# A two-headed sequence kernel: the shift weights' cast and the small diagonals moved from GpSimd to VectorE, with a new order of all steps

## The chip, the cores and the metric

The kernel runs on one core of a Trainium2 chip. The core has five engines that run side by side: TensorE (matmuls), VectorE, ScalarE, GpSimd and SyncE, which here only starts transfers. The metric is the device time of one execution in microseconds (us); smaller is better. The profiled span of an execution is about 1.8 us shorter than its timed value (259.0 against 260.8 us before). Runs are called fast or slow by their time and by the clock that was granted to TensorE, and only fast runs are compared.

## The reference

The output is the concatenation of two independent layers, each over 2048 time steps and 640 channels in bf16.

```python
# Part A: diagonal state space model (complex, 640 states)
Lam_bar = exp(dt * (Lambda_re + 1j * Lambda_im))
B_bar   = ((Lam_bar - 1) / Lam)[:, None] * (B_re + 1j * B_im)
h[t]    = Lam_bar * h[t-1] + B_bar @ x[t]            # t = 0 .. 2047
y[t]    = 2 * real(C @ h[t]) + Dskip * x[t]
# Part B: a short convolution, a gate, a long convolution, a gate
k_shift = sum over j in 0..3 of shift_k[:, j] * k delayed by j
kv      = k_shift * v
y       = irfft(rfft(kv padded to 4096) * rfft(ssm_k padded))[:2048] + ssm_D * kv
out_b   = q * y
out     = concatenate([out_a, out_b], axis=-1)
```

## The kernel before

Both parts are cut into small steps, and one long string, `ORDER`, says in which sequence they are issued. Each name is a Python generator. Each time that the name occurs, the generator advances by one step, and the instructions that the step emits are chained in that order on their engine. An engine therefore runs its instructions strictly in the order of the string. An instruction that waits holds up everything behind it on the same engine.

```python
last, running, traced, at = {}, {}, nc.cur_bb.bb.instructions, 0
for name in ORDER.split():
    if name not in running:
        kind = name.rstrip("0123456789")
        running[name] = makers[kind](*(int(d) for d in name[len(kind):])) or iter(())
    next(running[name], None)
    for ins in traced[at:]:
        if last.get(ins.engine, ins) is not ins:
            tc.add_manual_dep(ins, last[ins.engine].name, ...)      # cut
        last[ins.engine] = ins
    at = len(traced)
```

The step names that matter below are these.

- Part A: `xt` turns x, `dg` makes small diagonal matrices, and `bt` and `lb` turn rows of B plainly and through those diagonals. `m(c,j)` is a block: 20 matmuls of 128x512 and a scan on VectorE, for time half c and state group j. `c` scales C, and `k` makes the constant matrix K0. `p(c,i,e)` is an output product: about 30 matmuls, one evacuation of PSUM on ScalarE and one store. It needs nothing more from VectorE.
- Part B, for each of five channel groups G: `v` convolves on VectorE, `sh` and `sk` are the first transform stage, `h` and `f` the spectra (with the products on VectorE), `z` goes back, `zt` or `zp` turns, `y` finishes and multiplies by q, and `st` stores. `R`, `g` and `Mq` build the transform constants, and `tb` builds tables.

The four places that the change touches:

```python
def start(self):                                   # Part B, first thing on GpSimd
    g = self.nc.gpsimd
    g.memset(self.dtap[:], 0.0)
    ...                                            # cut: one small load
    sk_b = self.small.tile([128, 5, 4], bf16, name="sk_b")
    g.dma_start(out=sk_b[:], in_=self.B_shift_k.rearrange("(g c) j -> c g j", c=128))
    g.tensor_copy(out=self.sk[:], in_=sk_b[:])     # waits here for the load above

def make_dg(self, j):                              # three 128x128 diagonals of row j
    eng = self.nc.vector if j == 0 else self.nc.gpsimd
    for i, v in enumerate((self.ndim, self.dre, self.dim)):
        eng.tensor_scalar_mul(out=self.dg[:, j, i, :], in0=self.ident[:], scalar1=v[:, j:j + 1])

def turn_lb(self, j):                              # uses them on TensorE
    ...
            nc.tensor.matmul(pl[:, k - k0, :], lhsT=bre[:, ks], rhs=dg[:, 1:3, :], start=True, stop=False)
            nc.tensor.matmul(pl[:, k - k0, :], lhsT=bim[:, ks], rhs=dg[:, 0:2, :], start=False, stop=True)
    ...

# ORDER: first line ... last two lines (553 steps in all)
# xl0 bl3 xl1 g0 bl2 bl4 R kl0 rot g0 dg0 dg2 bt3 cl Mq dg1 R rot tb2 bt3 Mq dg3 tb2 Mq xt3 bl0 xt2 gs xt3 ...
# p101 f44 z42 p101 z41 z43 z42 ql4 p110 z43 zp40 p110 zp41 zp40 zp42 p110 zp41 zp43 zp42 p111 zp43 y41 p111 y40 y41 p130 p111 y40 st4 p131
# p130 p130 p120 p131 p131 p121 p120 p120 p121 p121
```

The last two lines show that before ends with eleven steps of output products alone (behind `st4`).

## Time and profile before

Four runs of before gave 260.18, 260.52, 261.64 and 782.32 us; the last one is counted as slow.

| stretch of the profiled run, us | length | TensorE busy | VectorE busy | what sets the pace |
|---|---|---|---|---|
| 0 to 30.4 | 30.4 | 9.6 | 9.7 | waits for constants and diagonals |
| 30.4 to 64.9 | 34.6 | 25.0 | 28.6 | blocks, one late row of B |
| 64.9 to 95.5 | 30.6 | 28.1 | 30.0 | VectorE |
| 95.5 to 240 | 144.5 | 135.3 | 118.1 | mostly TensorE |
| 240 to 259 | 19.0 | 15.4 | 2.4 | TensorE alone |

These are the first lines of the profile page of before: busy time of each engine, then the busy tenths of 40 equal slices of the span, then each engine's share of the chain of waits that ended last (in before this chain could be followed back only to 95.5 us, so its shares add up to 62% of the span). PE is TensorE, PEld its weight loads, DVE VectorE, ACT ScalarE, POOL GpSimd.

```profile
PE 213.4 (82%) x2207; PEld 160.0 (62%) x2207; DVE 188.7 (73%) x355; ACT 168.9 (65%) x232; POOL 40.9 (16%) x89
...
PE   0223949668999787999999999999997899799994
...
POOL 4099994332021000000000000000000000000000
...
PE 31%; DVE 23%; ACT 5%; issue 3%; DVEq 0%; ACTq 0%
```

TensorE starts late (twos in the first slices, where GpSimd is at 9) and is full at the end. The windows of before, from which the table is taken, give the stretch in this form: length, then busy time of PE, PEld, DVE, ACT and POOL with instruction counts, then granted clock, DMA share and GB/s.

```profile
95.50:240.00 144.50, 135.29 (x1591) 107.61 (x1591) 118.08 (x212) 99.96 (x117) 0.22 (x2) 1.00 0.67 141
```

The start is explained by GpSimd's timeline in before (start, duration, engine, line, operation, result and sources; in brackets the idle time before it and what ended it).

```profile
2.98 0.91 POOL L575 DMA_DIRECT2D sk_b<-in_B_shift_k_dram  x1
12.67 0.20 POOL L576 CAST sk<-sk_b 128x20 f32<-128x20 bf16 x1 [8.78 <-DMA sk_b<-in_B_shift_k_dram]
...
16.47 0.61 POOL L334 TENSOR_SCALAR dg<-ident,ndim 128x128 bf16<-128x128 bf16 x1
...
32.60 2.02 POOL L334 TENSOR_SCALAR dg<-ident,ndim 128x128 bf16<-128x128 bf16 x1
34.60 2.05 POOL L334 TENSOR_SCALAR dg<-ident,dre 128x128 bf16<-128x128 bf16 x1
36.64 1.60 POOL L334 TENSOR_SCALAR dg<-ident,dim 128x128 bf16<-128x128 bf16 x1
```

GpSimd stands still for 8.78 us before a cast of 0.20 us, because it waits for a load that it started itself. A diagonal takes 0.6 us there, and the last three (row 4) take 1.6 to 2.05 us. The timeline of TensorE in before shows who pays for this.

```profile
23.77 0.37 PE L356 MATMUL pl<-dg,nat_re 128*128 128x256 bf16 x1 [9.37 <-POOL dg L334]
...
30.37 1.25 PE L468 MATMUL ps<-xe_110,BT 128*128 128x512 bf16 x5 [0.52 <-DVE xe_110 L316]
...
38.30 0.27 PE L356 MATMUL pl<-dg,nat_re 128*128 128x256 bf16 x1 [3.42 <-POOL dg L334]
```

TensorE waits 9.37 and 3.42 us for diagonals, and the first matmul of a block starts at 30.37 us. The end of before, in the timeline of ScalarE, is the evacuation of the last output product; its store follows, and the span ends at 259.0.

```profile
255.51 0.69 ACT L541 CAST yo<-ps 128x640 bf16<-128x640 f32 x1 [3.38 <-PE ps L537]
```

Three marks are used: the start of the first 128x512 block matmul (30.4 us in before), of the first K0 product on TensorE (69.3) and of the first spectrum product on VectorE (95.5). What is left from the third mark to the end is called *the rest*; in before it is 259.0 - 95.5 = 163.5 us.

### The profile page before, as it was taken

What the parts mean: (1) busy time and instruction counts of PE and PEld (TensorE: products, weight loads), DVE (VectorE), ACT (ScalarE), POOL (GpSimd) and SP (SyncE); (2) the same over time, 40 slices, a digit from 0 to 9 for tenths busy, and PEclk for the clock granted to TensorE, in tenths of its full rate; (3) what the DMA queues carried; (4) which work ended last, traced back from release to release, by engine and by line L of the source; (5) the groups of instructions that cost most, each with busy time, mean ns of one, the idle gap of its engine ahead of it and who ended that gap; (6) DMA issues with size and microseconds to landing.
All of it is one profiled execution on the core that took longest, in us unless ns stands there. A gap on an engine that the chain in (4) does not pass through costs nothing.

```text
span 259.0 us, 5361 instructions
## 1 busy us (share of the span) xinstructions
PE 213.4 (82%) x2207; PEld 160.0 (62%) x2207; DVE 188.7 (73%) x355; ACT 168.9 (65%) x232; POOL 40.9 (16%) x89
## 2 busy tenths in 40 slices
PE   0223949668999787999999999999997899799994
PEld 0212724334576576666778788876956788688772
DVE  3312793998999999999999459769899991942300
ACT  5045627998769888675546288767977998464221
POOL 4099994332021000000000000000000000000000
PEclk9999999968999999999999999999999999999999
DMA  5989908100007999691099450699579469171321
GB/s 155 213 176 242 244 8 209 34 1 3 0 0 103 194 205 220 143 210 35 25 262 192 113 132 3 196 180 219 112 153 230 109 132 188 41 172 37 89 71 51
DMA packets 101760, 33.03 MB, mean 127 GB/s; under 512 B 97256, under 2 KB 100584, under 8 KB 101736
## 3 DMA queue, kind: packets, MB, share of 16 engines
q1 hardware_dynamic: 101636, 32.68, 59.7%
q8 instruction: 17, 0.28, 0.5%
q0 software_dynamic: 80, 0.01, 0.2%
q14 instruction: 7, 0.06, 0.1%
q10 hardware_dynamic: 20, 0.00, 0.0%
HBM read 10.82 MB, written 7.86 MB: 72 GB/s over the span
## 4 chain that ended last, share of the span: by engine, by line
PE 31%; DVE 23%; ACT 5%; issue 3%; DVEq 0%; ACTq 0%
PE ps L524 15%; DVE pr L492 4%; PE ps L537 3%; DVE pw L683 3%; DVE pw L684 2%; DVE tap L640 2%; DVE tap L646 2%; DVE po L481 2%; DVE pr L481 2%; ACT Xs L679 2%; DVE Y L685 1%; ACT Hf L665 1%; DVE qin L744 1%; DVE Y L686 1%; PE ps L587 1%
## 5 line engine op out<-in xcount | busy, mean ns | idle before, releaser
L524 PE MATMUL ps<-C_183,h 128*128 128x320 bf16 x320 | 48.4, 299 | 1.3 <-DVE qin L744 0.7
L524 PEld LDWEIGHTS <-h 128*128 128x128 bf16 x320 | 30.4, 98 | 12.4 <-issue 1.8
L541 ACT CAST yo<-ps 128x640 bf16<-128x640 f32 x16 | 11.1, 694 | 33.5 <-PE ps L537 15.6
L679 ACT CAST Xs<-ps 128x1024 bf16<-128x1024 f32 (+1 forms) x25 | 21.8, 895 | 5.6 <-DVE pw L684 5.4
L589 ACT CAST As_h<-ps 128x1024 bf16<-128x1024 f32 x20 | 19.4, 1033 | 4.0 <-PE ps L587 4.0
L665 ACT CAST Hf<-ps 128x1024 bf16<-128x1024 f32 (+1 forms) x25 | 20.8, 910 | 1.2 <-PE ps L608 1.1
L716 ACT CAST Zs<-ps 128x1024 bf16<-128x1024 f32 x20 | 19.8, 1038 | 1.8 <-PE ps L714 1.8
L683 DVE TENSOR_TENSOR pw<-Xs,Hf 128x1024 bf16<-128x1024 bf16 (+1 forms) x25 | 15.2, 607 | 7.4 <-ACT Xs L679 7.4
L589 ACT CAST As_kv<-ps 128x1024 bf16<-128x1024 f32 x20 | 19.2, 1062 | 1.5 <-PE ps L587 1.5
L646 DVE TENSOR_TENSOR tap<-tap 128x2048 bf16<-128x2048 bf16 x15 | 19.1, 1273 | 0.5
L468 PEld LDWEIGHTS <-BT 128*128 128x128 bf16 x100 | 9.7, 100 | 14.7 <-issue 3.4
L470 PEld LDWEIGHTS <-BT 128*128 128x128 bf16 x100 | 10.0, 100 | 12.6 <-issue 1.4
L605 PE MATMUL ps<-As_h,Gre 128*128 128x128 bf16 x75 | 16.4, 219 | 1.7 <-ACT Hf L665 1.1
L474 ACT CAST z<-ps 128x1024 bf16<-128x1024 f32 x10 | 10.1, 1014 | 11.1 <-PE ps L470 11.1
L356 PE MATMUL pl<-dg,nat_re 128*128 128x256 bf16 x25 | 6.6, 300 | 12.8 <-POOL dg L334 12.8
L711 PE MATMUL ps<-Y,Hre 128*128 128x128 bf16 x75 | 16.4, 219 | 0.3 <-ACT As_kv L589 0.3
L608 PE MATMUL ps<-As_kv,Gre 128*128 128x128 bf16 x75 | 16.4, 219 | 0.0
L605 PE MATMUL ps<-As_kv,Gre 128*128 128x128 bf16 x75 | 16.4, 219 | 0.0
L607 PE MATMUL ps<-As_kv,Gim 128*128 128x128 bf16 x75 | 16.4, 219 | 0.0
L606 PE MATMUL ps<-As_kv,nGim 128*128 128x128 bf16 x75 | 16.4, 219 | 0.0
L714 PE MATMUL ps<-Y,Hre 128*128 128x128 bf16 x75 | 16.4, 219 | 0.0
L608 PE MATMUL ps<-As_h,Gre 128*128 128x128 bf16 x75 | 16.4, 219 | 0.0
(234 smaller groups left out, 652.3 us busy)
## 6 DMA issues: line engine op xcount, KB each, us to landing
h_st<-in_B_ssm_k_dram SPq DMA_DIRECT2D x5, 512.0 KB, 4.7
qin<-in_B_q_dram SPq DMA_DIRECT2D x5, 512.0 KB, 6.7
kv_d<-vT SPq DMA_DIRECT2D x5, 512.0 KB, 3.1
kv_st<-kv_d SPq DMA_DIRECT2D x5, 512.0 KB, 4.0
out_dram<-yo SPq DMA_DIRECT2D x16, 160.0 KB, 1.8
out_dram<-qin SPq DMA_DIRECT2D x5, 512.0 KB, 4.0
nat_re<-in_A_B_re_dram SPq DMA_DIRECT2D x5, 160.0 KB, 4.5
nat_im<-in_A_B_im_dram SPq DMA_DIRECT2D x5, 160.0 KB, 4.8
```

The source lines that it names most:

```text
L524: nc.tensor.matmul(py[:, b, 0:320], lhsT=h[:, s, hs], rhs=self.C4[:, 2 * e + s, j, c0:c0 + 320], start=(j == 0 and s == 0), stop=False)
L589: nc.scalar.copy(out=As[:, :, 32 * pr:32 * pr + 32], in_=pf.rearrange("p (c k) -> p k c", k=32))
L605: nc.tensor.matmul(pt[:, 0, cs], lhsT=C.Gre[:, k1, :], rhs=As[:, r, :], start=True, stop=False)
L606: nc.tensor.matmul(pt[:, 0, cs], lhsT=C.nGim[:, k1 - 1, :], rhs=As[:, im, :], start=False, stop=True)
L607: nc.tensor.matmul(pt[:, 1, cs], lhsT=C.Gim[:, k1, :], rhs=As[:, r, :], start=True, stop=False)
L608: nc.tensor.matmul(pt[:, 1, cs], lhsT=C.Gre[:, k1, :], rhs=As[:, im, :], start=False, stop=True)
L646: nc.vector.tensor_tensor(out=acc[:], in0=acc[:], in1=t[:], op=ALU.add)
L665: nc.scalar.copy(out=S["Hf"][:, :, pos * 128:(pos + n) * 128], in_=pt[:, :, 0:n * 128])
L679: nc.scalar.copy(out=Xs[:, :, 0:W], in_=pt[:, :, 0:W])
L683: nc.vector.tensor_tensor(out=pw[:, 0, :, 0:W], in0=Xs[:, :, 0:W], in1=Hf[:, :, hs], op=ALU.mult)
L711: nc.tensor.matmul(o_re, lhsT=C.Hre[:, k1, :], rhs=ypl(k1, 0), start=True, stop=False)
L716: nc.scalar.copy(out=Zs[:, :, 8 * qd:8 * qd + 8], in_=pzf.rearrange("p (k c) -> p c k", k=8))
```

## The change

Its intent is to get GpSimd's chain of waits off the start: the small loads are issued first, index rows (iotas) follow while they fly, the cast of the shift weights becomes a step `sc` of VectorE, and the 12 diagonals of rows 1 to 4 join those of row 0 on VectorE. Some of Part A's scalars come later, and the whole string of steps is new.

```diff
 ORDER = """
-xl0 bl3 xl1 g0 bl2 bl4 R kl0 rot g0 dg0 dg2 bt3 cl Mq dg1 R rot tb2 bt3 Mq dg3 tb2 Mq xt3 bl0 xt2 gs xt3 lb3 bl1 xt2 xt3 hl0 xt2 bt2 lb3 xt1
+xl0 bl0 xl1 bl4 kl0 g0 R Mq g0 bl1 rot dg0 Mq bl3 bt0 rot dg2 dg1 lb0 tb0 cl Mq bt0 R Mq gs tb0 lb0 xt3 xt1 sc xt3 xt3 xt4 dg3 bl2 xt0 xt1
 ...   (all 553 steps reordered to 556; cut)
-p101 f44 z42 p101 z41 z43 z42 ql4 p110 z43 zp40 p110 zp41 zp40 zp42 p110 zp41 zp43 zp42 p111 zp43 y41 p111 y40 y41 p130 p111 y40 st4 p131
-p130 p130 p120 p131 p131 p121 p120 p120 p121 p121
+f41 f40 y31 p111 f41 y30 f42 p111 y31 f43 p111 f42 f44 z40 st3 f43 f42 p110 z40 f44 f43 z41 p110 f44 z42 p110 z41 z43 ql4 z42 p130 z43 zp40
+p130 zp41 zp40 zp42 p130 zp41 zp43 zp42 zp43 y40 y40 y41 y41 st4
 """
@@ make_dg @@
-        eng = self.nc.vector if j == 0 else self.nc.gpsimd
         for i, v in enumerate((self.ndim, self.dre, self.dim)):
-            eng.tensor_scalar_mul(out=self.dg[:, j, i, :], in0=self.ident[:], scalar1=v[:, j:j + 1])
+            self.nc.vector.tensor_scalar_mul(out=self.dg[:, j, i, :], in0=self.ident[:], scalar1=v[:, j:j + 1])
@@ g_scalars @@
+        yield                                     # diagD later
         self.diagD = self.const.tile([128, NT, 128], bf16, name="diagD")
@@ PartB.start @@
-        g.tensor_copy(out=self.sk[:], in_=sk_b[:])
+    def cast_sk(self):                            # step "sc"
+        self.nc.vector.tensor_copy(out=self.sk[:], in_=self.sk_b[:])
@@ kernel body @@
     C.start()
+    pb.start()
     pa.preamble()
-    pb.start()
+    C.iotas()                                     # index rows gathered in one method
```

Cut: the moves of iotas into one method, one iota removed, and one more `yield` in `Mq`.

More of the change, by code (lines that the diff above doesn't have):

```diff
@@ L32 @@
 ORDER = """
-xl0 bl3 xl1 g0 bl2 bl4 R kl0 rot g0 dg0 dg2 bt3 cl Mq dg1 R rot tb2 bt3 Mq dg3 tb2 Mq xt3 bl0 xt2 gs xt3 lb3 bl1 xt2 xt3 hl0 xt2 bt2 lb3 xt1
-bt2 bt4 xt1 xt1 lb2 bt4 xt4 lb2 xt0 xt4 tb1 ql0 xt0 xt4 xt0 v0 dg4 tb1 m02 R tb3 v0 tb3 v0 lb4 g2 m02 m03 v0 lb4 m02 v0 g2 m02 m04 c40 tb0
-c00 c40 c20 c40 lb1 c00 c30 c00 c01 lb1 m02 bt1 c01 bt0 c20 bt1 tb0 kl1 c01 m01 c20 c10 g1 c30 c30 m03 c31 g1 bt0 lb0 c41 c21 g4 c31 lb0 m01
-c31 m00 c41 c10 c10 c21 c11 c41 c11 ht0 c21 k4 m01 g4 c11 k2 g3 k4 m01 m00 g3 k3 m01 g5 k2 sh00 k3 sh01 m00 sh02 sh00 sh03 sh02 v0 m00 k0 g5
@@ L37 @@
-tb4 sh03 H k1 sh01 m00 tb4 v1 sk00 k0 sk01 sk00 sk02 sk01 v1 late xb1 sk03 sk02 h00 sk03 v1 h01 h00 k1 f00 v1 hl1 h01 f01 m03 f00 v1 f02 f01
-f03 m04 f04 f00 h02 h02 f01 h03 f02 h04 f03 f02 z00 h03 h04 f03 f04 z01 z00 xb1 z01 m10 f04 m03 kl2 z02 m10 ht1 m03 sh10 z02 z03 sh11 sh10
-sh12 m10 sh13 z03 v1 m14 sh13 zt0 m10 sh11 sh12 m10 h10 m14 h11 m04 h10 h12 h11 h13 m04 h12 h14 m13 h13 h14 m04 sk10 m13 sk11 v2 p011 sk11
-sk10 v2 y01 p011 v2 y00 sk12 p011 sk13 sk12 hl2 y01 p001 sk13 y00 v2 st0 m14 v2 f10 p001 f11 f10 p001 ht2 m14 sh20 f11 f12 sh20 f13 f14 f10
@@ L41 @@
-ql1 p021 kl3 f12 f11 f13 f12 p020 p021 p021 f14 f13 p010 p020 p020 f14 sh21 sh22 sh21 sh23 v2 p000 sh23 sh22 p010 p010 h20 m14 p000 h21 h20
-p000 h22 h21 v3 h23 h22 h24 sk20 h23 sk21 sk22 h24 sk21 p030 v3 sk22 sk20 v3 z10 p030 z11 v3 p030 z10 z12 m13 z11 v3 z13 z12 sk23 p031 m13
-z13 hl3 sk23 zt1 m13 kl4 f20 p031 f21 f20 f22 ht3 f21 f20 f23 p031 f24 m11 f22 f21 f23 f22 sh30 f24 f23 sh31 m11 sh32 sh33 sh30 f24 v3 y11
-sh32 m11 z20 sh31 z21 sh33 y11 y10 z20 h30 y10 z21 h31 h30 m11 st1 h32 h31 h33 h32 h34 z22 m11 h33 sk30 h34 sk31 z22 sk32 v4 sk33 sk31 hl4
@@ L45 @@
-z23 sk32 ql2 m12 sk33 v4 sk30 z23 v4 zt2 f30 ht4 v4 m12 f31 f30 m12 f32 v4 f31 f33 f34 f30 sh40 sh40 sh41 f32 f31 sh42 sh41 sh43 sh42 f32
-y21 f33 v4 z30 sh43 f33 z31 f34 z30 y20 z31 f34 z32 y21 h40 z32 z33 y20 h40 h41 z33 m12 st2 h42 h41 zt3 h43 h42 h44 m12 h43 sk40 sk41 sk40
-sk42 sk43 sk41 ql3 p100 sk43 sk42 h44 f40 p100 f41 f40 p100 f42 f41 f40 y30 y31 f43 f42 f41 f44 y30 f43 z40 y31 p101 z40 f42 st3 f44 f43 z41
-p101 f44 z42 p101 z41 z43 z42 ql4 p110 z43 zp40 p110 zp41 zp40 zp42 p110 zp41 zp43 zp42 p111 zp43 y41 p111 y40 y41 p130 p111 y40 st4 p131
@@ L49 @@
-p130 p130 p120 p131 p131 p121 p120 p120 p121 p121
+xl0 bl0 xl1 bl4 kl0 g0 R Mq g0 bl1 rot dg0 Mq bl3 bt0 rot dg2 dg1 lb0 tb0 cl Mq bt0 R Mq gs tb0 lb0 xt3 xt1 sc xt3 xt3 xt4 dg3 bl2 xt0 xt1
+xt1 hl0 xt4 xt2 xt4 dg4 tb1 ql0 bt4 xt0 xt0 xt2 lb4 xt2 bt4 gs tb1 m00 lb4 v0 tb4 bt1 v0 m00 lb1 R tb4 m04 bt1 v0 tb2 lb1 tb2 v0 m00 lb3 v0
+tb3 m04 bt3 lb3 m01 m00 tb3 g2 c40 c40 bt3 bt2 c30 c40 lb2 bt2 c20 m03 c30 c30 c10 c20 c20 c00 c10 c10 c00 m03 kl1 c00 g2 ht0 k2 m00 g5 lb2
+m03 sh00 k2 sh01 sh00 k0 m03 sh01 g5 sh02 sh03 m03 v0 g1 k0 k4 sh02 sh03 m04 g1 k3 m04 g4 m01 k4 sk00 k3 sk01 m02 g4 m04 g3 sk01 m01 sk00 g3
@@ new lines @@
+sk02 m01 sk03 k1 hl1 sk03 H m02 h00 m01 sk02 h01 k1 h02 h00 m02 h03 h01 h04 f00 h02 ht1 late xb1 m02 f01 h03 h04 sh10 f00 f02 f01 f03 sh10
+m02 sh11 sh12 sh11 sh13 sh12 f00 p000 sh13 f02 f01 f04 p010 p000 c41 f03 p000 v1 c41 z00 p010 v1 p030 p010 z00 xb1 c41 c21 m11 p030 v1 c21
+p030 v1 c11 v1 c21 m10 c11 c01 f02 m11 c01 kl2 c11 z01 f04 f03 m10 m14 z01 f04 v1 c31 c01 c31 m10 z02 z03 z02 m10 h10 z03 h11 h10 zt0 h12
+m10 m14 h13 h11 h14 p020 h12 v2 h13 h14 v2 sk10 p020 sk11 sk12 sk10 p020 sk13 v2 m12 sk11 hl2 sk13 v2 sk12 m11 v2 y00 y01 m12 c31 f10 y00
@@ new lines @@
+f11 f10 kl3 f12 y01 f11 f13 ht2 f10 sh20 p031 sh20 f11 f12 st0 f13 f12 f14 sh21 p031 sh22 sh21 p031 sh23 f13 v2 p021 sh23 sh22 m11 f14 f14
+z10 p021 m11 h20 p021 z10 h21 ql1 h20 h22 v3 h21 z11 h22 h23 z11 h24 z12 v3 h23 sk20 h24 z13 sk20 v3 sk21 z12 sk22 sk23 sk22 v3 hl3 m13 sk21
+m14 v3 sk23 z13 m14 zt1 f20 m13 f21 ht3 m14 f20 f22 kl4 f21 f23 f20 f24 p001 f22 f21 f23 f22 z20 p001 y10 z20 sh30 p001 y10 sh31 f24 sh30
+sh32 f23 sh33 p011 sh31 v3 sh33 f24 sh32 m13 h30 p011 m13 h31 h30 p011 h32 h31 h33 h32 m13 h34 y11 h33 sk30 sk31 h34 sk30 y11 sk32 sk33 sk31
@@ new lines @@
+m12 st1 z21 hl4 sk33 z22 sk32 z23 m12 z21 f30 z23 f31 m12 f32 f30 ql2 f31 f33 z22 f34 f30 p101 zt2 ht4 f32 f31 f33 f32 sh40 p101 p100 sh40
+p101 v4 f34 sh41 p100 sh42 v4 sh43 sh41 p100 p121 sh43 v4 sh42 v4 z30 p121 f33 v4 z31 p121 z30 y20 z31 y21 f34 z32 y21 z33 z32 v4 h40 y20
+z33 h41 h40 st2 h42 zt3 h41 h43 h42 h44 p120 h43 h44 sk40 p120 sk41 sk42 sk40 p120 sk43 ql3 p131 sk41 sk42 sk43 f40 p131 f41 f40 p131 y30
+f41 f40 y31 p111 f41 y30 f42 p111 y31 f43 p111 f42 f44 z40 st3 f43 f42 p110 z40 f44 f43 z41 p110 f44 z42 p110 z41 z43 ql4 z42 p130 z43 zp40
@@ L59, in __init__ @@
         g.iota(self.pidx_i[:], pattern=[[0, 1]], base=0, channel_multiplier=1)
-        self.c20 = tpool.tile([128, 1], i32, name="c20")
-        g.iota(self.c20[:], pattern=[[0, 1]], base=2 ** 20, channel_multiplier=0)
         self.c27 = tpool.tile([128, 1], i32, name="c27")
@@ L68, in _cos, with _iota @@
         self.nc.scalar.activation(out=out_ap, in_=aph[:], func=ACT.Sin, bias=self.hpi[:, 0:1], scale=-1.0)
-    def _kq_iota(self, shape, pat_slot, pat_part, tag):
-        g, tp = self.nc.gpsimd, self.tp
-        kcol = tp.tile(shape, i32, name=f"{tag}_kcol")
-        g.iota(kcol[:], pattern=pat_slot, base=0, channel_multiplier=0)
-        q8 = tp.tile(shape, i32, name=f"{tag}_q8")
-        g.iota(q8[:], pattern=pat_part, base=0, channel_multiplier=0)
-        return kcol, q8
+    def _iota(self, name, shape, pattern, base=0):
+        t = self.tp.tile(shape, i32, name=name)
+        self.nc.gpsimd.iota(t[:], pattern=pattern, base=base, channel_multiplier=0)
+        return t
     def _split(self, bits, tag):
@@ L89, in build_R @@
         sh = [128, 16, 2]
-        kcol, q8 = self._kq_iota(sh, [[1, 16], [0, 2]], [[0, 16], [8, 2]], "r")
-        g.iota(kcol[:, 0:1, 1:2], pattern=[[0, 1], [0, 1]], base=16, channel_multiplier=0)
-        g.iota(q8[:, 0:1, 1:2], pattern=[[0, 1], [0, 1]], base=0, channel_multiplier=0)
-        a_i, mask = self.a_i, self.r_mask
+        kcol, q8, a_i, mask = self.r_kcol, self.r_q8, self.a_i, self.r_mask
         def bc(t):
@@ L113, in start @@
         nc, tp, g = self.nc, self.tp, self.nc.gpsimd
-        gcol = tp.tile([128, 8], i32, name="r_gcol")
-        g.iota(gcol[:], pattern=[[1, 8]], base=0, channel_multiplier=0)
+        gcol = self._iota("r_gcol", [128, 8], [[1, 8]])
         self.a_i, c_i = self._split(4, "r")
@@ L123, in start, with iotas @@
         self.nGim = self.cpool.tile([128, 15, 128], bf16, name="nGim")
+    def iotas(self):
+        g = self.nc.gpsimd
+        self.r_kcol = self._iota("r_kcol", [128, 16, 2], [[1, 16], [0, 2]])
+        self.r_q8 = self._iota("r_q8", [128, 16, 2], [[0, 16], [8, 2]])
+        g.iota(self.r_kcol[:, 0:1, 1:2], pattern=[[0, 1], [0, 1]], base=16, channel_multiplier=0)
+        g.iota(self.r_q8[:, 0:1, 1:2], pattern=[[0, 1], [0, 1]], base=0, channel_multiplier=0)
+        self.m_acol = self._iota("m_acol", [128, 16], [[1, 16]])
+        self.m_ccol = self._iota("m_ccol", [128, 4], [[1, 4]])
     def build_G(self, i):
@@ L170, in build_Mq @@
         v.tensor_scalar_mul(out=coef[:], in0=coef[:], scalar1=1.0 / NFFT)
-        acol = tp.tile([128, 16], i32, name="m_acol")
-        g.iota(acol[:], pattern=[[1, 16]], base=0, channel_multiplier=0)
-        ccol = tp.tile([128, 4], i32, name="m_ccol")
-        g.iota(ccol[:], pattern=[[1, 4]], base=0, channel_multiplier=0)
+        acol, ccol = self.m_acol, self.m_ccol
         mask = tp.tile([128, 4], f32, name="m_mask")
@@ L397, in g_scalars @@
             self.gs.append((re, nre, nim))
+        yield
         self.diagD = self.const.tile([128, NT, 128], bf16, name="diagD")
@@ L438, in table_setup @@
         nc, g = self.nc, self.nc.gpsimd
-        cmul = tp.tile([128, NT], i32, name="tb_cmul")
-        g.iota(cmul[:], pattern=[[0, NT]], base=TC, channel_multiplier=0)
         phc = tp.tile([128, NT], i32, name="tb_phc")
-        g.tensor_tensor(out=phc[:], in0=cmul[:], in1=self.Fi[:], op=ALU.mult)
+        g.tensor_tensor(out=phc[:], in0=self.cmul[:], in1=self.Fi[:], op=ALU.mult)
         yield
@@ L573, in start @@
             g.dma_start(out=self.dtap[0:128:16, :], in_=self.B_ssm_D.rearrange("(o c) -> c o", c=8))
-        sk_b = self.small.tile([128, 5, 4], bf16, name="sk_b")
-        g.dma_start(out=sk_b[:], in_=self.B_shift_k.rearrange("(g c) j -> c g j", c=128))
-        g.tensor_copy(out=self.sk[:], in_=sk_b[:])
+        self.sk_b = self.small.tile([128, 5, 4], bf16, name="sk_b")
+        g.dma_start(out=self.sk_b[:], in_=self.B_shift_k.rearrange("(g c) j -> c g j", c=128))
+    def cast_sk(self):
+        self.nc.vector.tensor_copy(out=self.sk[:], in_=self.sk_b[:])
     def stage1(self, G, kind, pr):
@@ L790 @@
     C.start()
+    pb.start()
     pa.preamble()
-    pb.start()
+    C.iotas()
     pa.dg = tpool.tile([128, NT, 3, 128], bf16, name="dg")
-    pa.lo_idx = tpool.tile([128, CW], i32, name="tb_lo")
-    nc.gpsimd.iota(pa.lo_idx[:], pattern=[[2, CW]], base=0, channel_multiplier=0)
+    pa.cmul = C._iota("tb_cmul", [128, NT], [[0, NT]], TC)
+    pa.lo_idx = C._iota("tb_lo", [128, CW], [[2, CW]])
     def late():
@@ L805 @@
         "m": pa.block, "p": pa.project, "R": C.build_R, "g": C.build_G, "H": C.build_H, "Mq": C.build_Mq, "late": late,
-        "sh": lambda G, q: pb.stage1(G, "h", q), "sk": lambda G, q: pb.stage1(G, "kv", q), "hl": pb.load_h, "ht": pb.tap_d, "kl": pb.load_kv,
+        "sh": lambda G, q: pb.stage1(G, "h", q), "sk": lambda G, q: pb.stage1(G, "kv", q), "hl": pb.load_h, "ht": pb.tap_d, "sc": pb.cast_sk, "kl": pb.load_kv,
         "ql": pb.load_q, "v": pb.conv, "h": pb.h_spec, "f": pb.spec, "z": pb.back, "zt": pb.turn_z, "zp": pb.turn_zp, "y": pb.final, "st": pb.store,
```

## The prediction

> **What bounds it now.** TensorE, behind a late start. The page gives TensorE 82% busy, VectorE 73%. By stretches (windows view) TensorE is busy 9.6 of the first 30.4 us, 25.0 of the next 34.6, 94% from 95.5 to 240 us, and full from 240 to 255.5. From 65 to 95.5 us VectorE is: 30.0 of 30.6.
>
> Why late (timeline, waits): GpSimd issues two small loads at 1.8 and 3.0 us, then waits 8.8 us, in order, at the cast of the shift weights, until 12.67. Everything of GpSimd comes after: phases, constants of R and Mq, and 12 small diagonals, 0.60 us each, the last three 1.6 to 2.05 us. TensorE waits for diagonals twice, 9.4 and 3.4 us. The slow ones coincide with the first convolution on VectorE: the Trainium skill ("SBUF — State Buffer", section "SBUF: two separate sides") says VectorE and GpSimd take a shared port pair as an exclusive lock; 0.60 against 2.0 us agrees.
>
> **The change.** The cast leaves GpSimd, so those 8.8 us go. The diagonals run on VectorE at 0.21 to 0.25 us (its first three in the trace): about 7.2 + 5.7 us leave GpSimd, some 2.5 us go to VectorE, idle then. GpSimd's scalars (20 x 0.2 us) still come before C is needed.
>
> **Walk of the start, with the trace's durations (estimate).** x's second half landed at 12.94 and is issued after the same bytes: no gain there. Five turns of x, 0.86 us each cold, 0.45 warm: to 16.5; bt4 and lb4 to 18.5; the first 128x512 block matmul at 19 us instead of 30.4. Then m00, m04, m01, m03 at 4.3 us each with the turns of B between them; B's rows 1 and 3 land near 21, C near 30. VectorE does the convolution, one block and the C products (5 x 1.35 us) by 42. So the first K0 product starts near 43 us instead of 69.3, but before had m02 done there too (4.3 us): a lead of about 22 us. First spectrum product on VectorE near 75, before 95.5.
>
> **What is given back.** There VectorE still has conv 1 and the second C scaling to do, about 15 us that before had done: about 132 us left against 120. From 95.5 to 240 it was 82% busy; at 82 to 88% it needs 150 to 161 us. TensorE's remaining work at its former 91% issue rate needs 156. Both end near 231. The tail is worse: before ended in output products needing only TensorE, 3.5 us after the last matmul (0.69 evacuation, 1.8 landing); now turns of Z, both y products, 1.2 us of VectorE and a 512 KB store of 4.0 us: about 6 us after the last matmul plus 2 us of holes. About 241 profiled; timed runs are 1.8 us longer.
>
> **Prediction:** 243 us, range 236 to 252; faster by over 2% 0.93, within 2% 0.05, slower 0.02.
>
> **Right if:** GpSimd shows no wait for the shift weights; no diagonal waits on TensorE; first block matmul at 17 to 22 us; first K0 product at 40 to 48; TensorE busy near 213, VectorE near 191; last matmul to end 5 to 8 us.
>
> **Wrong if:** B's rows land later than 21 us, behind k and v; ScalarE (C scaling, tables) holds PSUM from 30 to 60 us; VectorE becomes the limit from 75 us on, over 90% full; the new order, with p spread out, starves TensorE late.

## The result, and the profile after

| | before | after |
|---|---|---|
| timed, median (us) | 261.08 | 231.74 (231.73 to 231.76, four runs) |
| ratio of fast runs | 1 | 0.8887, 95% interval 0.8854 to 0.8919 |
| profiled span | 259.0 | 230.0 |
| first block matmul | 30.4 | 18.8 |
| first K0 product | 69.3 | 43.9 |
| first spectrum product | 95.5 | 75.0 |
| the rest | 163.5 | 155.0 |

A ratio here is the mean time of one kernel's fast runs over the mean of the other's fast runs of the same rounds, so it isn't quite the ratio of the medians quoted. The forecast of 243 us was too high, and the result lies below its range of 236 to 252.

The same lines of the page, now of after:

```profile
PE 208.0 (90%) x2199; PEld 159.4 (69%) x2207; DVE 193.4 (84%) x368; ACT 168.3 (73%) x232; POOL 31.3 (14%) x75
...
PE   0399998799998999999999998999999999999980
...
POOL 8796360222210000000000000000000000000000
...
PE 65%; DVE 16%; ACT 13%; issue 2%; DMA 1%; DVEq 1%; ACTq 0%
```

TensorE is at 7 or more, mostly at 9, from the third slice nearly to the end. The two chain lines can't be set side by side, since before's covers only the time from 95.5 us to the end. Over the rest alone, summed from the pieces of the chain, TensorE has 79 of 163.5 us in before and 118 of 155.0 in after, VectorE 60 and 1. The timelines of GpSimd, VectorE and TensorE in after, in this order, answer to the lines of the start that were shown for before.

```profile
2.91 0.90 POOL L572 DMA_DIRECT2D sk_b<-in_B_shift_k_dram  x1
3.81 0.23 POOL L70 IOTA r_kcol<- 128x32 int32 x1
...
9.27 1.04 POOL L452 TENSOR_TENSOR tb_ph<-tb_lo,Fi 128x512 int32<-128x512 int32 x1
```

```profile
9.24 1.11 DVE L332 TENSOR_SCALAR dg<-ident,ndim 128x128 bf16<-128x128 bf16 x1
10.28 0.24 DVE L332 TENSOR_SCALAR dg<-ident,dre 128x128 bf16<-128x128 bf16 x1
...
14.11 0.23 DVE L575 CAST sk<-sk_b 128x20 f32<-128x20 bf16 x1
```

```profile
10.73 0.37 PE L354 MATMUL pl<-dg,nat_re 128*128 128x256 bf16 x1 [0.95 <-DVE dg L332]
...
18.82 1.24 PE L465 MATMUL ps<-xe_110,BT 128*128 128x512 bf16 x4
```

GpSimd goes on at 3.81 with iotas, without a wait; a diagonal takes 0.24 us on VectorE; and the cast comes at 14.11 without a wait of its own. The longest wait of TensorE for a diagonal in these lines is 0.95 us. It is for a diagonal that took 1.11 us instead of 0.24, and that ends at 10.35, just as GpSimd's product at 9.27 ends (10.31). This is the port lock of the prediction in the other direction. The Trainium skill ("SBUF — State Buffer", section "SBUF: two separate sides") says that the lock goes to whichever of the two starts first; 1.11 against 0.24 us agrees that VectorE can be the one that loses. (VectorE's record starts 0.03 us earlier here, so the recorded starts don't tell who got the pair; the ends do. The same happens once more in after and twice in the run *dg0first* below: a diagonal of 1.01 to 1.13 us beside a GpSimd product of 1.03 or 1.04 us, which ends 0.04 or 0.05 us before it.)

The windows of after show the second half of the gain.

```profile
75.00:222.50 147.50, 145.09 (x1670) 115.14 (x1673) 121.63 (x211) 105.37 (x126) 0.33 (x3) 1.00 0.68 146
```

From 75 to 222.5 us TensorE is idle for only 147.5 - 145.1 = 2.4 us; in before it was idle for 144.5 - 135.3 = 9.2 us between the third mark and 240. But idle time is only part of the 8.5 us by which the rest is shorter. After's rest also holds 45 matmuls fewer (1690 weight loads against 1735) and 146.0 us of TensorE's work against 150.7: the new order does that much more before the third mark. So 4.7 us of the 8.5 are work done earlier; 6.5 are fewer holes before the last matmul; and a longer time after the last matmul takes 2.8 back. The end of after in the timelines of TensorE, VectorE and SyncE:

```profile
222.76 2.36 DVE L742 TENSOR_TENSOR qin<-ps,qin 128x1024 bf16<-128x1024 f32 x2 [0.38 <-PE ps L739]
223.23 0.41 PE L739 MATMUL ps<-Mq,Zt 128*128 128x64 bf16 x8 [0.28 <-ACT Zt L730]
225.14 0.38 SPq L746 DMA_DIRECT2D out_dram<-qin  x1
```

The last matmul ends at 223.64, two multiplications on VectorE and one store follow, and the span ends at 230.0, 6.4 us later.

### The profile page after: what moved, and what is told of

Read it like the earlier page. It is cut to its first block, busy times and chain, and to the rows that moved or that the text cites. A ratio compares the mean times of both kernels' runs of the same rounds, so it can differ in the third digit from the quotient of the medians.

```text
span 230.0 us, 5354 instructions
## 1 busy us (share of the span) xinstructions
PE 208.0 (90%) x2199; PEld 159.4 (69%) x2207; DVE 193.4 (84%) x368; ACT 168.3 (73%) x232; POOL 31.3 (14%) x75
## 4 chain that ended last, share of the span: by engine, by line
PE 65%; DVE 16%; ACT 13%; issue 2%; DMA 1%; DVEq 1%; ACTq 0%
PE ps L521 19%; PE ps L428 6%; PE ps L467 6%; PE ps L465 6%; PE ps L585 5%; PE ps L534 5%; ACT Hf L663 4%; ACT Zs L714 3%; ACT As_kv L587 3%; PE ps L606 2%; PE ps L604 2%; PE ps L603 2%; PE ps L605 2%; DVE tap L644 2%; DVE C_185 L417 2%
## 5 line engine op out<-in xcount | busy, mean ns | idle before, releaser
L521 PEld LDWEIGHTS <-h 128*128 128x128 bf16 x320 | 30.4, 98 | 12.6 <-issue 2.1
L538 ACT CAST yo<-ps 128x640 bf16<-128x640 f32 x16 | 11.1, 692 | 26.7 <-PE ps L530 10.0
L467 PEld LDWEIGHTS <-BT 128*128 128x128 bf16 x100 | 9.8, 98 | 11.8
L604 PE MATMUL ps<-As_h,nGim 128*128 128x128 bf16 x75 | 16.4, 219 | 0.0
L605 PE MATMUL ps<-As_h,Gim 128*128 128x128 bf16 x75 | 16.4, 219 | 0.0
L606 PE MATMUL ps<-As_kv,Gre 128*128 128x128 bf16 x75 | 16.4, 219 | 0.0
L710 PE MATMUL ps<-Y,nHim 128*128 128x128 bf16 x75 | 16.4, 219 | 0.0
L711 PE MATMUL ps<-Y,Him 128*128 128x128 bf16 x75 | 16.4, 219 | 0.0
```

What stands on the lines that cost most here:

```text
L467: nc.tensor.matmul(pz[:, i, :], lhsT=self.BT[:, j * NT + k, 2 + i, :], rhs=xo[:, k, PAD - 1:PAD - 1 + CW], start=False, stop=(k == NT - 1))
L521: nc.tensor.matmul(py[:, b, 0:320], lhsT=h[:, s, hs], rhs=self.C4[:, 2 * e + s, j, c0:c0 + 320], start=(j == 0 and s == 0), stop=False)
L604: nc.tensor.matmul(pt[:, 0, cs], lhsT=C.nGim[:, k1 - 1, :], rhs=As[:, im, :], start=False, stop=True)
L605: nc.tensor.matmul(pt[:, 1, cs], lhsT=C.Gim[:, k1, :], rhs=As[:, r, :], start=True, stop=False)
L606: nc.tensor.matmul(pt[:, 1, cs], lhsT=C.Gre[:, k1, :], rhs=As[:, im, :], start=False, stop=True)
```

## The experiments

Two questions stood open: which part of the change shortens the start by how much, and why the rest is 8.5 us shorter when the prediction had it slightly longer. The ideas at stake, in words:

- *Cast, diagonals or order*: the start is won by taking the cast off GpSimd, by taking the diagonals off it, or only by the new order.
- *Spread products against start only*: either the rest is shorter because the new order puts output products, which need TensorE almost alone, where TensorE would otherwise wait; or the rest is shorter merely because the earlier start leaves less to do.
- *Port lock*: diagonals on GpSimd are slow when VectorE's convolution runs beside them.

The expectations are quoted; the text after each says in words what hit and what missed. All twelve kernels gave correct results, and all had before run on the same chip in the same rounds. "Old order" is before's string with the new steps inserted (`sc`, the moved cast, ahead of the first `v0`, one more `gs`, Part A's scalars, one more `Mq`).

### The parts alone and together

**u_both**: after, with cast and diagonals put back on GpSimd. Only the new order (and the iotas' place) is left.

```diff
+        g.tensor_copy(out=self.sk[:], in_=self.sk_b[:])        # in PartB.start
-        self.nc.vector.tensor_copy(out=self.sk[:], in_=self.sk_b[:])
-            self.nc.vector.tensor_scalar_mul(out=self.dg[:, j, i, :], ...
+            (self.nc.vector if j == 0 else self.nc.gpsimd).tensor_scalar_mul(out=self.dg[:, j, i, :], ...
```

> The new order, with the cast of the shift weights back on GpSimd behind its load and the diagonals of rows 1 to 4 back on GpSimd. Theory S (the start is gated by GpSimd: wait of 8.8 us plus 12 diagonals): GpSimd stands still until about 12.7 us, the last diagonals are ready near 30, the first block matmul starts near 31 us instead of 18.8, and the whole is 241 to 247 us: about half of the gain is lost. Rival O (the new order made the gain, the moved operations are small change): 232 to 236 us.

Measured: 248.21 us median, ratio 0.9528 (0.946 to 0.9597). The profile of this kernel fell in the slow state (mean clock 0.92), so its span isn't compared, and the median includes that one slow run (252.85); the other three lie between 247.6 and 248.5, a little above what was expected. The order alone is worth 4.7%, somewhat less than half of the 11.1% of the whole change, so theory S fits and the rival doesn't.

**o_all**: all the code of after with the old order.

```diff
-(ORDER of after)
+(ORDER of before, with sc, one gs and one Mq inserted)
```

> All moved operations, but the old order of the steps. Theory S: the first block matmul comes near 20 us instead of 30.4 and the time is 241 to 249 us. If the moved operations alone make the gain: 231 to 236 us. Rival O: 256 to 261 us, as before.

Measured: 247.91 us, ratio 0.9516 (0.945 to 0.9583), inside the forecast of theory S. Marks 19.6, 54.8 and 81.0, rest 163.6. The pieces alone are worth 4.8%. The product of the two ratios, 0.9528 x 0.9516 = 0.907, is 1.8 points above the 0.8887 of the whole change: order and pieces help each other. The rest tells more than the time: with the old order it is 163.6, as long as in before, although the start is 14.5 us shorter.

**u_cast**: after, with only the cast put back on GpSimd (the first two lines of u_both's edit).

> Changed kernel, only the cast of the shift weights back on GpSimd behind its load. Theory S: GpSimd waits until about 12.7 us, all its work is 8.8 us later, VectorE waits for its iotas; first block matmul 24 to 27 us, time 236 to 241 us. Rival (the diagonals were the gate, as the waits of the kernel before name them): under 234 us.

Measured: 236.21 us, ratio 0.9088 (0.9021 to 0.9156), inside the forecast. The first block starts at 21.9, two us earlier than the forecast, since GpSimd waits 6.1 us here and not 8.8: the load landed at 9.9 us. The rest is 155.0.

**u_diag**: after, with only the diagonals of rows 1 to 4 put back on GpSimd (the last two lines of that edit).

> Changed kernel, only the diagonals of rows 1 to 4 back on GpSimd. Theory S with the cast's wait gone: GpSimd has time for them, first block matmul 19 to 20.5 us, time 232 to 235 us. Rival (the diagonals were the gate): first block matmul 25 us or later, time 238 to 243 us.

Measured: 240.94 us, ratio 0.9249 (0.9187 to 0.931), and this forecast missed: the diagonals are worth 3.6 points in the new order, more than the cast (2.0). The first block starts at 27.0, 8.2 us later than in after. The timeline of GpSimd in u_diag shows where.

```profile
19.73 1.49 POOL L332 TENSOR_SCALAR dg<-ident,ndim 128x128 bf16<-128x128 bf16 x1
21.21 2.06 POOL L332 TENSOR_SCALAR dg<-ident,dre 128x128 bf16<-128x128 bf16 x1
23.25 1.60 POOL L332 TENSOR_SCALAR dg<-ident,dim 128x128 bf16<-128x128 bf16 x1
```

The waits view of the same kernel (engine, line, what it waited for: us in total, times, longest) has the price.

```profile
PE pl L354 <- POOL dg L332: 6.1, 1, 6.1
```

Row 4's diagonals take 5.2 us together instead of three times 0.6, and TensorE waits 6.1 us for them. VectorE begins the convolution at 19.54, so the lock suggested itself; the run *lock* below tests it.

**o_cast**: the old order with only the cast moved (the iotas stay early, as in after).

> Old order, only the cast moved (and the iotas early); diagonals of rows 1 to 4 on GpSimd as before. If GpSimd is the serial gate of the start, everything of it comes 8.9 us earlier: first block matmul near 21.5 us, first spectrum product 87 to 89 us instead of 95.5, and the rest after it unchanged at 163.5 us: 252 to 255 us. If the diagonals alone gate the start: above 257 us.

Measured: 250.62 us, ratio 0.9643 (0.9595 to 0.9691), slightly better than the 252 to 255 us that were expected. Marks 21.6, 60.7 and 86.9, rest 163.6.

**o_diag**: the old order with only the diagonals moved (the iotas where after has them, so behind the cast).

> Old order, only the diagonals moved to VectorE; cast still on GpSimd behind its load. GpSimd starts at 12.7 us as before, but has 12.9 us less to do: first block matmul near 22 us, first spectrum product 85 to 88 us, rest 163.5 us: 250 to 253 us. If the wait for the shift weights alone gates the start: above 257 us.

Measured: 253.84 us, ratio 0.9766 (0.9707 to 0.9824): clearly below 1, but the interval holds the 2% line, so whether it is over 2% stays unclear. The forecast missed: the time is a little above 250 to 253 us, the first block starts at 28.1, not near 22, and the third mark comes at 88.8, not at 85 to 88. With the cast left on GpSimd, which here ran at 13.17 after a wait of 9.36 us, the iotas behind it come late too, and VectorE itself then stands before a diagonal: it waits 4.80 us for the index row of the mask of `Mq`. Moving the diagonals passed most of the wait on.

What follows from the eight corners (two orders, cast moved or not, diagonals moved or not; all but before have after's place of the iotas): in the old order the cast is worth 3.6%, the diagonals 2.3%, both 4.8%. In the new order undoing the cast costs 2.0 points, undoing the diagonals 3.6, undoing both 6.4.

| kernel | order | third mark | span | rest |
|---|---|---|---|---|
| before | old | 95.5 | 259.0 | 163.5 |
| o_cast | old | 86.9 | 250.5 | 163.6 |
| o_diag | old | 88.8 | 252.3 | 163.5 |
| o_all | old | 81.0 | 244.6 | 163.6 |
| u_cast | new | 78.1 | 233.1 | 155.0 |
| u_diag | new | 84.7 | 239.7 | 155.0 |
| after | new | 75.0 | 230.0 | 155.0 |

The table rejects the idea that the rest is shorter because the start is earlier. Starts differ by up to 14.5 us within the old order and by 9.7 us within the new one, and the rest moves by 0.1 us at most. Only the order moves it, by 8.5 us. The windows of the rest agree: TensorE's work there is 150.5 to 150.7 us in before, o_cast and o_all, and 146.0 in u_cast, u_diag and after.

### Spread products, taken back

**p_late**: after up to the step `sk40`, with the output products of the second time half taken out of it, then the old order for what is left.

```diff
-(ORDER of after: p101 p100 p121 p120 p131 ... spread among the steps of groups 3 and 4)
+(the same start without any p1..; from sk40 on the old order, all p1.. in it)
```

> Changed kernel; from the fifth group's second stage on, the order of the kernel before, so all eight output products of the second half of the sequence come in the last part, as before, instead of filling TensorE's holes. First spectrum product unchanged at 75.0 us. Theory P (the new order's rest is shorter, 155 against 163.5 us, because the products are spread): the rest grows to 159 to 164 us, time 236 to 241 us. Rival (other changes of the order do it): within 2 us of 231.7, the shorter tail making up for some.

Measured: 242.0 us, ratio 0.9298 (0.9263 to 0.9334). Marks 19.0, 44.1 and 75.2, as in after; rest 165.5. Theory P forecast a rest of 159 to 164 and 236 to 241 us; both came out a little higher, far from the rival's 231.7. So 10.5 us of rest come back with the old tail.

**p_end**: the smallest form of the same: only the four products p100, p101, p120 and p121 leave their places and go to the very end.

```diff
-... p101 zt2 ht4 ... p101 p100 sh40 p101 v4 f34 sh41 p100 ... p121 ... p120 ... st4
+... zt2 ht4 ... sh40 v4 f34 sh41 ... st4 p101 p101 p100 p101 p100 p121 p100 p121 p120 p121 p120 p120
```

> Changed kernel; only the four products p100, p101, p120, p121 (about 14 us of TensorE) are taken from the middle of the order and put behind everything else. Theory P: TensorE stands idle in the middle and the 14 us come back in full at the end less the 6 us of the last store that they now cover: 236 to 241 us. Rival (VectorE's or ScalarE's chain does not let the steps move up, but TensorE has slack anyhow): under 233 us.

Measured: 241.02 us, ratio 0.926 (0.9226 to 0.9294). Marks 18.8, 43.9 and 75.0, rest 164.4; the time is at the upper edge of theory P's forecast. The move of four of the sixteen products costs 9.4 us of span. Part of that is trivial: work put behind everything else adds its length. What counts is how little the remainder gained: its last matmul ends at 221.7 us, only 2.0 us earlier than in after, though the four products, which then run for another 14.1 us, are gone from it. So after had hidden about 12 of these 14 us. The time after the last matmul is 2.8 us shorter in p_end, which leaves the 9.4. The windows of after, then of p_end, for the stretch that the four products left:

```profile
160.00:180.00 20.00, 19.43 (x255) 16.80 (x253) 19.73 (x34) 16.15 (x20) 0.00 (x0) 1.00 0.73 149
180.00:200.00 20.00, 20.00 (x258) 17.10 (x256) 9.25 (x14) 15.42 (x19) 0.00 (x0) 1.00 0.69 163
```

```profile
160.00:180.00 20.00, 17.19 (x256) 15.63 (x253) 19.72 (x35) 18.75 (x22) 0.00 (x0) 0.91 0.71 140
180.00:200.00 20.00, 15.04 (x163) 13.12 (x160) 9.14 (x14) 10.99 (x13) 0.00 (x0) 0.83 0.69 157
```

From 120 to 160 us, and at all three marks, the two kernels agree to within 0.1 us. From 160 to 180 VectorE is full in both (19.7 of 20 us), so it sets the pace, and TensorE has time to spare; in p_end VectorE stays busy until 189 us, past the hole shown below. In after the four products fill it; in p_end TensorE goes idle, its clock falls to 0.91 and 0.83, and the products cost full length at the end. The timeline of TensorE in p_end shows the largest hole.

```profile
185.99 0.27 PE L709 MATMUL ps<-Y,Hre 128*128 128x128 bf16 x1 [4.71 <-DVE Y L683]
...
186.60 0.31 PE L709 MATMUL ps<-Y,Hre 128*128 128x128 bf16 x1
```

After an idle time of 4.71 us the 128-wide products take 0.31 us and start 0.11 us apart, where in after they take 0.22 us and start 0.06 us apart at the same place. The Trainium skill ("TensorE: Matmul & The Clock Gate", section "What's actually happening") says that the clock falls to half after an idle window of about 3.4 us and comes back after about as long a busy one; 4.71 us of idle and 0.11 against 0.06 us between starts agree with the fall. The return took longer here: the products stay slow until 192.1 us, for 6.1 us. And so long a hole isn't needed: from 175.3 to 178.4 us the same trace shows the slow pace after holes of only 1.55 and 1.22 us. A hole that is filled thus saves twice: the hole, and the slow matmuls behind it. Busy time shows the second part: 212.9 us in p_end for the same matmuls as 207.8 us in dg0first below (both traces have all 2207 records). Within the rest, 5.2 us of the 9.4 are slower matmuls and 7.0 are holes, less the 2.8 us after the last matmul.

The advice exists in general form. The Trainium skill ("Perfetto Trace Analysis", section "Optimization Strategy") says that a kernel whose most-contended engine changes over time may gain from interleaving those regimes. This agrees: 9.4 us for four products.

### The port lock

**lock**: u_diag with the first convolution moved behind `bt1`, so that VectorE runs no convolution while GpSimd makes row 4's diagonals.

```diff
-m00 lb4 v0 tb4 bt1 v0 m00 lb1 R tb4 m04 bt1 v0 tb2
+m00 lb4 tb4 bt1 m00 lb1 R tb4 m04 bt1 v0 v0 v0 tb2       (diagonals on GpSimd as in u_diag)
```

> As u_diag (diagonals of rows 1 to 4 on GpSimd), but the first convolution's steps are moved behind the second transposed block row of B, so that VectorE runs no tap while GpSimd makes the diagonals of row 4. Theory L (the shared port pair slows them): row 4's diagonals take 0.6 us each instead of 1.5, 2.06 and 1.6; they are ready near 21.6 us instead of 24.85, the first block matmul starts near 23 us instead of 27.0. Rival (GpSimd is slow there for a reason of its own): 1.5 us or more each and a first block near 27 us. The time of the whole is not forecast (the convolution is late): 236 to 243 us.

Measured: the timeline of GpSimd in this kernel, for the same three diagonals as shown for u_diag, is this.

```profile
19.71 0.60 POOL L332 TENSOR_SCALAR dg<-ident,ndim 128x128 bf16<-128x128 bf16 x1
20.28 0.60 POOL L332 TENSOR_SCALAR dg<-ident,dre 128x128 bf16<-128x128 bf16 x1
20.86 0.60 POOL L332 TENSOR_SCALAR dg<-ident,dim 128x128 bf16<-128x128 bf16 x1
```

They start at the same time as in u_diag (19.7 us), on the same engine, and take 0.60 instead of 1.49, 2.06 and 1.60 us; the first block starts at 23.6 instead of 27.0. So the convolution beside them was the cause. That it acts through the port lock is the account of the Trainium skill's page on SBUF (the section cited above), with which these times agree. Only the time of the whole, 236 to 243 us, was forecast a little too low. The kernel as a whole is slower than u_diag (243.93 us, ratio 0.9381, 0.935 to 0.9412): VectorE now waits 11.96 us at a copy that stands ahead of the convolution, and the third mark comes at 86.2. Moving work off a lock isn't free when every engine runs in order.

### Attempts to beat after

**dg0first**: the diagonals of row 0 ahead of the constants of `Mq`, so that the diagonal which took 1.11 us isn't awaited.

```diff
-xl0 bl0 xl1 bl4 kl0 g0 R Mq g0 bl1 rot dg0 Mq bl3
+xl0 bl0 xl1 bl4 kl0 g0 R dg0 Mq g0 bl1 rot Mq bl3
```

> Changed kernel, with the three diagonals of row 0 in front of VectorE's small constants of Mq, so before GpSimd's first table phase. They take 0.25 us each (the first took 1.11), are ready near 8.5 us, and the diagonal products follow the first transposes at 9.6 instead of 10.7. If x's second half has landed by 12 us, all moves up by 1.1 us: 230.5 to 231 us. If x's landing (12.9 in the kernel before) is the gate: 231.4 to 231.8 us.

Measured: 232.04 us, ratio 0.891 (0.8878 to 0.8943), the same as after, and above both forecasts. Marks 19.1 and 75.3. Row 0's diagonals now took 0.22 to 0.25 us, but TensorE's turn of B waited for the transfer of B's imaginary row until 9.91 us, and two other diagonals met the lock (1.08 and 1.13 us). In after the same transfer was waited for only until 8.64 us, so in this trace its later landing hides what the edit may have won. The five runs spread from 230.97 to 232.49 us; a gain is not shown, nor is it ruled out.

**tail**: the last load of q goes early into the dead buffer of k, the finish of group 3 is issued while the last group's evacuation runs, and one output product (p130) is put behind the last `y`, under its store.

```diff
-... sk43 ql3 p131 sk41 sk42 sk43 f40 p131 ... z43 ql4 z42 p130 z43 zp40 p130 ... zp43 y40 y40 y41 y41 st4
+... sk43 ql3 p131 sk41 sk42 sk43 ql4 f40 p131 ... z43 z42 y30 z43 y31 y30 y31 st3 p110 zp40 ... zp43 y40 y41 y40 p130 y41 st4 p130 p130
-    self.S[G]["qin"] = self.io.tile([128, 16, 128], bf16, name="qin")
+    self.S[G]["qin"] = self.io.tile([128, 16, 128], bf16, name="qin", tag="kT" if G == 4 else "qin")
```

> Changed kernel with a new last part: the last q is loaded early into the dead buffer of k; the fifth group's spectrum steps come together, y of the fourth group behind them fills the wait for the evacuation of Z, and the last output product p130 comes behind the last y, under the 4 us store. TensorE ends as before near 223.6 or 1 us sooner; the last store is issued near 222.5 instead of 225.1; span 227 to 228, time 228 to 230 us. If the store of y is not what ends the kernel: 231.5 or more.

Measured: 229.34 us, ratio 0.882 (0.8791 to 0.8848), inside the forecast; the last store of Part B is issued at 222.9 us, as was expected, instead of 225.1.

**tail_split**: the same, with the last multiplication by q and the last store of Part B cut in two halves of time.

```diff
+                for h0 in (0, 8):                    # group 4 only: multiply and store one half, then the other
+                    ...                              # two multiplications of 128x512
+                    nc.sync.dma_start(out=self.o2[h0 * 128:(h0 + 8) * 128, ...], in_=qin[:, h0:h0 + 8, :])
```

> As tail, with the last multiplication and store cut into two halves of the rows, so that the first half's store runs under the second half's multiplication. 0 to 1 us less than tail: 227.5 to 229.5 us, if the output product's store does not end last.

Measured: 229.16 us, ratio 0.8812 (0.8783 to 0.884). The interval lies wholly below that of after (0.8854 to 0.8919), so this version beats both kernels, by about 0.8% over after. After didn't run in the same rounds; *dg0first*, which equals it, did, and took 232.04 us. The time is inside the forecast. It isn't told apart from *tail*. Its end, in the timeline of SyncE and TensorE:

```profile
222.07 1.58 SPq L749 DMA_DIRECT2D out_dram<-qin  x2
...
224.01 0.30 PE L530 MATMUL ps<-diagD,xe 128*128 128x64 bf16 x3
```

TensorE is busy until 224.31 while Part B's last halves are stored, and the span ends at 227.9, 3.6 us after the last matmul instead of 6.4.

## Why the prediction was right or wrong

**Right: the start.** The walk forecast 19, 43 and 75 us for the three marks; measured were 18.8, 43.9 and 75.0. This doesn't look like luck, as the steps between hold too: the turns of x ended at 16.6 us (forecast 16.5) and `lb4` at 18.9 (18.5). GpSimd shows no wait for the shift weights. o_cast, o_diag and o_all show that both pieces take part: the cast alone brings the first block to 21.6 in the old order, the diagonals alone to 28.1, both together to 19.6. One sum was wrong without visible harm: "7.2 + 5.7 us" counts the last three diagonals twice. Nine of 0.6 us and three of 5.7 us in all are 11.1 us.

**Right, with a small exception: no diagonal waits on TensorE.** One wait of 0.95 us is left, from the lock in the direction that the prediction hadn't considered.

**Right: the tail after the last matmul.** Forecast 5 to 8 us, measured 6.4; the sum used 6 plus 2 for holes and so gave 1.6 us too many. VectorE's busy time was 193.4 (forecast near 191); TensorE's was 208.0 (forecast near 213).

**Wrong: the rest.** The step that failed is "TensorE's remaining work at its former 91% issue rate needs 156", followed by "Both end near 231" and the tail on top. Before's windows from 180 to 240 us give such a rate (18.19 + 17.88 + 18.51 of 60 us). Term by term:

| term of the sum | predicted | measured |
|---|---|---|
| third mark | 75 | 75.0 |
| TensorE's work after it | 142 (156 x 0.91) | 146.0 |
| rate at which it runs | 91% | 98% (146.0 of 148.6) |
| TensorE ends | 231 | 223.6 |
| VectorE's work after the mark | 132 | 124.0 |
| last matmul to end | about 8 | 6.4 |
| added on the way from 239 to "about 241" | 2 | no such term |
| span | 241 | 230.0 |

The rate was off by 7 points, which is 11.8 us at the measured work (146.0 / 0.91 = 160.4 against 148.6); the work was guessed too small by 4 us, which hid part of it. Together they are 7.4 us of the 11 missed; 1.6 are the tail and 2 are a rounding up that no term stood for. Not all 7 points are the new order's. From the third mark to its last matmul before was at 94% (150.7 of 159.9 us), as the prediction's own first paragraph has it for 95.5 to 240 us; the 91% were too low even for the old order. The step from 94 to 98% is what the new order did: the rate was read from the old order and applied to a new one whose purpose was to change it. The prediction feared that the spread products would starve TensorE late; the opposite happened. p_end and p_late show it: take four spread products out, and 9.4 us come back, with TensorE's holes and its falling clock in view. The table of rests shows that an earlier start doesn't do it. The 4.7 us of work that the new order does before the third mark are the other part of the shorter rest; the prediction had allowed for that part: its 156 us at 91% mean 142 us of work, less than before's 150.7.

**Wrong: what VectorE has left.** "About 15 us that before had done" was too much: 124.0 us were left after the mark against before's 118.1 + 2.4 = 120.4, so only 3.6 us net were pushed back. It would have mattered if VectorE had been the limit over the whole rest; it is only full in stretches, such as 160 to 180 us.

**Left open.** With the same pieces, the third mark is 81.0 us in the old order (o_all) and 75.0 in the new one. The trace suggests that the old order has VectorE do the second convolution and the second scaling of C before that mark and the new one after it; no run isolates this, so those 6 us are argued and not shown. Whether dg0first could gain something when B's row lands earlier is open too.

## What to carry to other kernels

When a change reorders the work, don't carry a utilization over from the old order: list the stretches where another engine sets the pace, and see whether the new order puts independent work of the waiting engine there. Keep work that needs one engine alone (here output products) as filling for those stretches instead of leaving it to the end; four such products were worth 9.4 us here. And in an engine that runs in order, never let an instruction wait right behind the load that it waits for: issue the load, then work that needs nothing, and let the consumer run on an engine that has other things to do first.

## What the Trainium skill lacked or had wrong

- "DMA: Bandwidth & Descriptors", section "Anatomy of one DMA — SWDGE (gpsimd) path", gives a fit of 2.0 us plus bytes over 436e3 for one such transfer. That makes about 2.0 us (an estimate from the page) for the 5 KB of shift weights. Measured from the start of the issue to the consumer's start were 9.7 us in before (2.98 to 12.67), 7 us in u_cast and 10.3 us in o_diag, with the large loads of the start in flight beside it. That these are the reason is likely, but no run isolates it. The fit has no term for other traffic, and the page's remarks on load give no size for a small load beside large ones.
- "SBUF — State Buffer", section "SBUF: two separate sides", has the lock right, but gives no size for it in a chain of short operations: here 0.60 us became 1.49 to 2.06 us for GpSimd, and 0.24 us became 1.11 us for VectorE.
- "Perfetto Trace Analysis", section "Optimization Strategy", names the interleaving of regimes, but no way to size it. Here four products, 14.1 us of TensorE, cost 9.4 us more at the end than in the holes: 7.0 us of holes and 5.2 of slow matmuls behind them, less 2.8 us after the last matmul.
